# Loading v through the casting software queue, with the transfers of three queues modelled in the planned order

## The chip, the cores and the metric

The kernel runs on one core of a Trainium2 chip. The core has five engines that work side by side, each through its own list of instructions, in that list's order: TensorE (PE, matrix products, with its weight loads shown as PEld), VectorE (DVE), ScalarE (ACT), GpSimd (POOL) and SyncE (SP). Transfers between the chip's memory and its on-chip buffer run on 16 DMA engines that all queues share. SP and ACT issue theirs through hardware queues (q1 and q10 in the profile), POOL through a software queue (q0), whose transfers may change the number type on the way. The metric is device time in microseconds (us), so less is better.

## What is computed

Two things follow each other. First comes a retention layer over q, k and v of shape (4 batches, 8 heads, 768 tokens, 64): a state per head decays by a factor gamma at each token and takes up the outer product of k and v, and q reads it:

```
state = gamma * state + outer(k[t], v[t])
y[t]  = scale * (q[t] @ state)
```

Its output, seen as x of shape (4, 768, 512), goes through an MLP mixer: a token MLP along the tokens (weights 768x256 and 256x768), added to x to give u, and then a channel MLP along the channels (weights 512x1536 and 1536x512), added to u:

```
u   = x + (relu(x^T w_tok1) w_tok2)^T
out = u + relu(u w_ch1) w_ch2
```

Inputs and output are float32. The kernel casts the operands of its matrix products to float16.

## The kernel before

**How the work is tiled.** A *pair* is two heads of one batch, so there are 16 pairs, four in each batch; they are counted from 0 in the order in which they are loaded. The retention of a pair runs in six chunks of 128 tokens. The *front* of a pair (function `front`) does this:

- k is cast to float16 and scaled by a per-token decay (L314 on ACT, L316 on DVE, one instruction a head); q and v are cast as they are (`cast`: L325 on POOL, L323 on ACT).
- k and q are transposed (`turn`). In batches 0 and 1 PE does it (L348) and ACT or DVE moves the result to kT or qT (L356); in batches 2 and 3 a DMA transpose on SP does it (L340).
- PE multiplies k by v for each chunk (L369); DVE accumulates the states (L378, L381), and two copies make them the float16 operand r (L392, L394).
- PE forms the scores of kT and qT, half a sequence at a time (L412); DVE masks them to am (L420).
- PE forms the output from r and qT (L434) and from am and v (L437); ACT or DVE scales it into X (L450, L454), and POOL or DVE casts it to x16 (L467).
- The token MLP follows: x16 by wt1 (L478), ReLU to h1 (L486), h1 by wt2 (L529), added to X (L537). From batch 1 on, u is cast (L545) and transposed to uT, by PE (L566) in batch 1 and by DMA on SP (L556) in batches 2 and 3. In batch 0 PE forms uT itself from wt2, h1 and x16 (L500, L503), and the addition to X comes later.

The *back* of a batch (function `back`) is the channel MLP, in two halves of 384 tokens. One half, a *set* here, is 48 products of wc1 and uT (L598), twelve ReLUs (L612, ACT), 36 products of wc2 (L625), three additions on DVE (L633) and three stores issued by ACT (L639). It needs uT of all four pairs of its batch.

**What sets the order.** Nothing runs while the program is written: every step is first recorded as an `Op` with the engines that could do it, its costs in ns as written in the code, what it depends on, the buffers and PSUM banks that it takes, and a priority. `arrange` (L77) is a list scheduler over these: it keeps a time for each engine, takes among the ops that could start earliest the one of the lowest priority tuple, gives it a start, an end and an engine, and so fixes each engine's list. Priorities of fronts start with 0, batch, pair, step (L297), those of backs with 1 (L587). For transfers it keeps one finish time for the software queue (`wire`) and one for the hardware queues (`ring`), at L139 to L150. PSUM banks 0 to 6 serve the fronts of batch 0, banks 0 to 4 later fronts, 5 to 7 the backs (`BANKS`, L53). Where the plan leaves PE empty in the first 30 us, matmuls on zeros are put in as fillers (L667 to L675).

**Loads.** `load` (L270) puts k, q and v of a pair on SP, as float32, in that order (L282; q of batches 0 and 1 by L279 in longer rows). Each has four buffers. A k or v load has 1536 rows of 256 bytes, so 96 for each DMA engine; q of the first two batches has 512 rows of 768 bytes. The weights are on POOL's software queue (`weight`, L255, issued by L257), which casts them to float16 on the way: wt1 (768 rows), wt2 (256 rows), wc1 and wc2 in three thirds each (512 rows a third). At L664, two of these issues are held back: wt1 until pair 3's q is cast, wc1's first third until pair 3's v is.

Of the kernel before, what the change touches and what calls it, by code (L numbers as in the profile page):

```python
# [17 lines left out]
def kernel(  # L18
# [11 lines left out]
    nc = tc.nc  # L30
# [19 lines left out]

    BUFS = dict(kf=4, qf=4, vf=4, k16=3, q16=3, v16=4, kT=4, qT=4, U=2, r16=3, am=8, X=3, x16=3, h1=4, u16=3,
                uT=3, h2=2, o=4)
# [11 lines left out]
    class Op:  # L64


        def __init__(self, prio, ways, deps=(), takes=(), uses=(), guard=0, dma=0, after=(), behind=None):
            self.prio, self.ways = prio, ways
            self.deps = [d for d in deps if d is not None]
            self.after = [d for d in after if d is not None]  # L70
            self.takes, self.guard, self.dma, self.behind = list(takes), guard, dma, behind
            self.end = self.eng = None
            for s in list(takes) + list(uses):
                s.users.append(self)
            ops.append(self)

    def arrange():  # L77
        free = dict(PE=0, ACT=2500, DVE=0, POOL=400, SP=700)
        wire, ring = [0], [0]
        taken = {t: [] for t in BUFS}  # L80
        bank_of = {i: None for i in range(8)}
        todo, order = list(ops), []

        def freed(slot):
# [6 lines left out]
        while todo:  # L91
# [47 lines left out]
            if op.dma:  # L139
                if eng == "POOL":  # L140
                    wire[0] = max(wire[0], start + 1200) + op.dma
                    op.end = wire[0] + 1000
                elif eng == "ACT":
                    ring[0] = max(ring[0], start + 800) + op.dma
                    op.end = start + 800 + 2 * op.dma + 1500
                else:

                    ring[0] = max(ring[0], start + 800, wire[0]) + op.dma
                    free["SP"] = max(free["SP"], ring[0] - 3600)
                    op.end = ring[0] + 750  # L150
            else:
                op.end = start + way[2]
# [96 lines left out]
    def request(prio, cost, emit, dma, takes=()):  # L249
        o = Op(prio, [("POOL", cost, cost, emit)], [], takes, dma=dma,  # L250
               after=queue[-8:-7], behind=queue[-1] if queue else None)
        queue.append(o)
        return o

    def weight(key, ns, dst, src):  # L255
        def emit():
            nc.gpsimd.dma_start(out=dst, in_=src.rearrange("(i p) j -> p i j", p=P))  # L257
        wops[key] = request((0, -1, 2), 850, emit, ns)

# [10 lines left out]
    def load(b, p):  # L270
        got = []
        for tag, src in (("kf", k), ("qf", q), ("vf", v)):
            s = Slot(tag)

            def emit(s=s, src=src, tag=tag):
                t = tile_of(s, [P, 2, NC, D], FP)
                r = src[b, 2 * p:2 * p + 2]
                if b < XB and tag == "qf":
                    nc.sync.dma_start(out=t.rearrange("p h (f i) d -> p h f (i d)", f=2),  # L279
                                      in_=r.rearrange("h (f p i) d -> p h f (i d)", f=2, p=P))  # L280
                else:
                    nc.sync.dma_start(out=t, in_=r.rearrange("h (c p) d -> p (h c) d", p=P))  # L282
            o = Op((0, b, p), [("SP", 100, 100, emit)], [], [s], dma=1150 if b < XB and tag == "qf" else 1720,
                   after=rows[-3:-2], behind=rows[-1] if rows else None)
            rows.append(o)
            got.append((s, o))
        loads[b, p] = got

    def front(b, p):
        first = b == 0  # L290
        FA = "first" if first else "front"
        n = [0]

        def op(ways, deps=(), takes=(), uses=(), late=0):
            n[0] += 1
            pe = ways[0][0] == "PE"
            pr = (late if late else 0, b, p, n[0])  # L297
            return Op(pr, ways, deps, takes, uses, guard=200 if pe and not first else 0)

# [4 lines left out]
        pc = slice(p * P, (p + 1) * P)  # L304
        (KF, kd), (QF, qd), (VF, vd) = loads[b, p]
        K, Q, V = Slot("k16"), Slot("q16"), Slot("v16")
        KT, QT = Slot("kT"), Slot("qT")

        def emit(e):
            t = tile_of(K, [P, NC, 2, D], F16)  # L310
            for j in range(2):
                h = 2 * p + j
                if e == "ACT":
                    nc.scalar.activation(t[:, :, j], KF.tile[:, j], AF.Copy, scale=gk[:, h:h + 1])  # L314
                else:
                    nc.vector.tensor_scalar(t[:, :, j], KF.tile[:, j], gk[:, h:h + 1], None, ALU.mult)  # L316
        kl = op(either(emit, ACT=(1100, 1180), DVE=(1020, 1080)), [kd, g_op], [K], [KF])

        def cast(slot, src, dep):
            def emit(e):  # L320
                t = tile_of(slot, [P, NC, 2, D], F16).rearrange("p c h d -> p h c d")
                if e == "ACT":
                    nc.scalar.copy(t, src.tile)  # L323
                else:
                    nc.gpsimd.tensor_copy(t, src.tile)  # L325
            ways = either(emit, POOL=(770, 860)) if first else either(emit, POOL=(770, 860), ACT=(780, 860))
            o = op(ways, [dep], [slot], [src])
            casts_of[b, p].append(o)
            return o
        ql = cast(Q, QF, qd)  # L330
        vl = cast(V, VF, vd)

# [3 lines left out]
        def turn(src, dst, dep):  # L336
            if b >= XB:
                def emit():
                    t = tile_of(dst, [P, S], F16)
                    nc.sync.dma_start_transpose(out=t.rearrange("d (c t) -> d c t", t=P),  # L340
                                                in_=flat(src.tile))
                return Op((0, b, p, 0), [("SP", 100, 100, emit)], [dep], [dst], [src], dma=800)
            T = Slot(FA)

            def emit():
                tp = tile_of(T, [P, 1024], F16)
                for c in range(NC):
                    nc.tensor.transpose(tp[:, c * P:(c + 1) * P], src.tile[:, c].rearrange("p h d -> p (h d)"), ident16)  # L348
            t = op(one("PE", (340, 500), emit), [dep, ident_op], [T], [src])

            def emit(e):
                d, o = tile_of(dst, [P, S], F16), T.tile[:, :S]
                if dst is QT:
                    d = d.rearrange("d (f p i) -> d f p i", f=2, i=HC)
                    o = o.rearrange("d (f i p) -> d f p i", f=2, i=HC)
                (nc.scalar.copy if e == "ACT" else nc.vector.tensor_copy)(d, o)  # L356
            return op(either(emit, ACT=act(S), DVE=dve(S, 1.04 if dst is QT else 0.54)),
                      [t], [dst], [T])
        kt = turn(K, KT, kl)
# [5 lines left out]
        def emit():  # L365
            st = tile_of(ST, [P, 512], FP)
            for c in range(NC - 1):
                for j in range(2):
                    nc.tensor.matmul(st[j * D:(j + 1) * D, c * D:(c + 1) * D], K.tile[:, c, j],  # L369
                                     V.tile[:, c, j], start=True, stop=True)  # L370
        pp = op(one("PE", (320, 470), emit), [kl, vl, two_before], [ST], [K, V])
        prev = None
# [29 lines left out]
        for hf in range(2):  # L402
            A = [Slot(FA), Slot(FA)]

            def emit(hf=hf, A=A):
                a = [tile_of(A[j], [P, 512], FP)[:, :HC * P].rearrange("p (i t) -> p i t", t=P)
                     for j in range(2)]
                for i in range(HC):
                    t = slice((hf * HC + i) * P, (hf * HC + i + 1) * P)
                    for j in range(2):  # L410
                        r = slice(j * D, (j + 1) * D)
                        nc.tensor.matmul(a[j][:, i], KT.tile[r, t], QT.tile[r, t],  # L412
                                         start=True, stop=True)
            a = op(one("PE", (300, 420), emit), [kt, qt, two_before], A, [KT, QT])
            for j in range(2):
# [8 lines left out]
        for hf in range(2):  # L424
            Y = Slot(FA)

            def emit(hf=hf, Y=Y):
                y = tile_of(Y, [P, 512], FP)
                R = RS.tile
                for i in range(HC):  # L430
# [5 lines left out]
                    for j in range(2):  # L436
                        nc.tensor.matmul(o[:, j * D:(j + 1) * D], AM[2 * hf + j].tile[:, i],  # L437
                                         V.tile[:, c, j], start=(c == 0), stop=(c == 0 or j == 1))
            y = op(one("PE", (360, 510), emit), am_ops[2 * hf:2 * hf + 2] + [r0, r1, vl], [Y],
# [112 lines left out]
        if b >= XB:  # L552
            def emit():
                if UT.tile is None:
# [3 lines left out]
            e = Op((0, b, p, 99), [("SP", 100, 100, emit)], casts + [None if opens else first_of[b, "uT"]],  # L558
                   [UT] if opens else [], [U16] if opens else [U16, UT], dma=900)
        else:  # L560
# [20 lines left out]
    def back(b):  # L581
        X, UT = Xs[b], UTs[b]
        seq = [0]

        def op(ways, deps=(), takes=(), uses=(), dma=0):
            seq[0] += 1
            return Op((1, b, seq[0]), ways, deps, takes, uses, dma=dma)  # L587
        for sh in range(2):
# [28 lines left out]
            for i in range(HC):  # L617
# [19 lines left out]
                def emit(sh=sh, i=i, O=O):  # L637
                    t0 = (sh * HC + i) * P
                    nc.scalar.dma_start(out=out[b, t0:t0 + P, :], in_=O.tile)  # L639
                op(one("ACT", (60, 60), emit), [ad], [], [O], dma=700)  # L640

    for p in range(NP):
        load(0, p)
    weight("t1", 1900, wt1, moe_w_tok1)
    weight("t2", 1900, wt2, moe_w_tok2)
    for i in range(NW):
        weight(("c1", i), 2600, wc1[i], moe_w_ch1[:, i * FW * P:(i + 1) * FW * P])
    for i in range(NW):
        weight(("c2", i), 2600, wc2[i], moe_w_ch2[i * FW * P:(i + 1) * FW * P])
    for b in range(1, B):  # L650
# [11 lines left out]
    for b in range(B):  # L662
        back(b)
    for key, o in (("t1", casts_of[0, 3][0]), (("c1", 0), casts_of[0, 3][1])):  # L664
        wops[key].deps.append(o)
    order = arrange()
    FILL, F_ON, F_NS = 0.7, 30000, 165  # L667
# [40 lines left out]
```

## Time and profile before

| what | value |
| --- | --- |
| time, median of 13 runs | 228.11 us (226.74 to 231.28) |
| the profiled execution's own time | 228.14 us |
| its span, first to last instruction | 226.2 us |
| PE busy | 203.6 us (90%), 1902 matmuls |
| DVE, ACT, POOL busy | 101.9, 110.4, 53.7 us (45%, 49%, 24%) |
| SP's and the weights' queue, share of 16 engines | q1 61.3%, q0 10.6% |
| outputs' queue | q10 7.8% |
| chain that ended last | PE 53%, DMA 28%, SP's issues 8% |

The span is shorter than the time, because starting and ending a program also counts in the time. A large busy share alone doesn't tell what a change is worth: PE's 90% holds 15.0 us of fillers (L675, 62 matmuls), and stretches in which PE ran at half clock. In a row such as `30.86 2.74 PE L478 MATMUL bank<-x,wt ... x24 [4.53 <-DMA wt<-...]` the numbers are the start, the time covered by the 24 instructions, and in brackets how long the engine was idle before and what ended that wait. In the chain of waits each piece is a start, a length and who held up the end in that stretch. In the slices a digit is the busy share in tenths of one fortieth of the span.

### The profile page before, as it was taken

To read this page: it belongs to the slowest core of one execution; us is meant where nothing else is said; L and a number is where in the kernel's file an instruction comes from. 1 tells how busy PE (TensorE), PEld (TensorE's weight loads), DVE (VectorE), ACT (ScalarE), POOL (GpSimd) and SP (SyncE) were. 2 spreads that over 40 slices of the span, in tenths; PEclk is the share of its full clock that TensorE was granted. 3 is DMA by queue.
4 is the path that set the end of the run, shared out by engine and by line. 5 is a ranking of instruction groups with operands and counts; after the bars stand their busy time and mean duration, and the time that the engine had idled before them with its cause. 6 is when DMAs were issued, how large, how long until landed. Compare 5 with 4: busy or idle time off the path is not lost.

```text
span 226.2 us, 4736 instructions
## 1 busy us (share of the span) xinstructions
PE 203.6 (90%) x1902; PEld 126.2 (56%) x1902; DVE 101.9 (45%) x266; ACT 110.4 (49%) x237; POOL 53.7 (24%) x94
## 2 busy tenths in 40 slices
PE   7987659399999988898699998999999999999993
PEld 3654457378776656665357655654554554645641
DVE  6377812359697858765377457402102102012021
ACT  4476817332889563755336743470460640722700
POOL 1344920303463454343323331300000000000000
PEclk9999967859999999999999999999999999999999
DMA  7999999999999999999999992411202102103012
GB/s 176 243 242 239 214 190 212 205 197 255 199 213 196 174 267 202 209 210 209 188 268 210 176 206 63 130 35 46 93 3 78 61 0 93 49 13 121 5 51 93
DMA packets 93206, 34.13 MB, mean 151 GB/s; under 512 B 81920, under 2 KB 90112, under 8 KB 93184
## 3 DMA queue, kind: packets, MB, share of 16 engines
q1 hardware_dynamic: 85504, 23.60, 61.3%
q0 software_dynamic: 4224, 3.93, 10.6%
q10 hardware_dynamic: 3456, 6.29, 7.8%
q8 instruction: 15, 0.25, 0.5%
q14 instruction: 7, 0.06, 0.1%
HBM read 26.74 MB, written 6.29 MB: 146 GB/s over the span
## 4 chain that ended last, share of the span: by engine, by line
PE 53%; DMA 28%; SPq 8%; POOL 3%; ACT 2%; issue 2%; DVE 2%; POOLq 0%; DVEq 0%; ACTq 0%
PE bank L598 23%; PE bank L625 19%; DMA qf<-in_q_dram 11%; DMA kf<-in_k_dram 7%; DMA qT<-q 7%; SPq L282 4%; PE bank L529 3%; PE bank L478 2%; DMA vf<-in_v_dram 2%; SPq L279 2%; PE bank L412 2%; SPq L340 2%; POOL v L325 1%; PE bank L348 1%; ACT h L612 1%
## 5 line engine op out<-in xcount | busy, mean ns | idle before, releaser
L612 ACT ACTIVATE h<-bank 128x384 f16<-128x384 f32 x96 | 46.1, 489 | 45.4 <-DVE o L633 32.0
L598 PE MATMUL bank<-uT,wc 128*128 128x384 f16 x384 | 68.2, 326 | 0.0
L625 PE MATMUL bank<-wc,h 128*128 128x512 f16 x288 | 67.2, 379 | 0.0
L598 PEld LDWEIGHTS <-wc 128*128 128x128 f16 x384 | 35.8, 98 | 22.1
L633 DVE TENSOR_TENSOR o<-X,bank 128x512 f32<-128x512 f32 x24 | 16.4, 685 | 67.8 <-PE bank L625 67.8
L625 PEld LDWEIGHTS <-h 128*128 128x128 f16 x288 | 26.8, 98 | 28.8 <-issue 0.3
L420 DVE TENSOR_TENSOR am<-bank,mask 128x384 f16<-128x384 f32 x64 | 33.0, 550 | 17.4 <-PE bank L412 17.0
L450 ACT ACTIVATE X<-bank,gy 128x192 f32<-128x192 f32 x44 | 15.6, 415 | 19.1 <-PE bank L437 11.5
L314 ACT ACTIVATE k<-kf,gk 128x384 f16<-128x384 f32 x28 | 15.7, 607 | 9.4 <-DMA kf<-in_k_dram 7.2
L537 DVE TENSOR_TENSOR X<-X,bank 128x384 f32<-128x384 f32 x32 | 16.1, 548 | 8.7 <-PE bank L529 8.2
L325 POOL CAST q<-qf 128x768 f16<-128x768 f32 x13 | 10.8, 829 | 36.3 <-DMA qf<-in_q_dram 34.0
L478 PE MATMUL bank<-x,wt 128*128 128x128 f16 x192 | 15.2, 237 | 4.5 <-DMA wt<-in_moe_w_tok_dram 4.5
L381 DVE SCALAR_TENSOR_TENSOR U<-U,gp,bank 128x64 f32<-128x64 f32 x64 | 17.7, 276 | 1.2
L467 POOL CAST x<-X 128x384 f16<-128x384 f32 x28 | 14.1, 511 | 13.5 <-DVE X L454 10.1
L478 PEld LDWEIGHTS <-wt 128*128 128x128 f16 x192 | 13.3, 107 | 6.5 <-DMA wt<-in_moe_w_tok_dram 4.7
L545 POOL CAST u<-X 128x384 f16<-128x384 f32 x23 | 11.3, 510 | 22.7 <-DVE X L537 22.7
L325 POOL CAST v<-vf 128x768 f16<-128x768 f32 x14 | 11.6, 830 | 18.7 <-DMA vf<-in_v_dram 14.2
L675 PE MATMUL bank<-zero 128*128 128x384 f16 x62 | 15.0, 379 | 1.2 <-DVE zero L205 1.2
L412 PE MATMUL bank<-qT,kT 64*128 64x128 f16 x192 | 10.0, 223 | 5.8 <-DMA qT<-q 5.2
L529 PE MATMUL bank<-h,wt 128*128 128x128 f16 x192 | 14.2, 225 | 0.0
L437 PE MATMUL bank<-v,am 128*128 128x64 f16 x192 | 13.5, 193 | 0.0
L529 PEld LDWEIGHTS <-wt 128*128 128x128 f16 x192 | 12.1, 101 | 2.2 <-issue 0.2
(57 smaller groups left out, 155.8 us busy)
## 6 DMA issues: line engine op xcount, KB each, us to landing
kf<-in_k_dram SPq DMA_DIRECT2D x16, 384.0 KB, 6.5
qf<-in_q_dram SPq DMA_DIRECT2D x16, 384.0 KB, 5.8
vf<-in_v_dram SPq DMA_DIRECT2D x16, 384.0 KB, 5.9
out_dram<-o ACTq DMA_DIRECT2D x24, 256.0 KB, 2.0
wc<-in_moe_w_ch_dram POOLq DMA_DIRECT2D x6, 512.0 KB, 18.5
wt<-in_moe_w_tok_dram POOLq DMA_DIRECT2D x2, 384.0 KB, 8.8
kT<-k SPq DMA_TRANSPOSE x8, 5.3
qT<-q SPq DMA_TRANSPOSE x8, 5.4
```

The lines of the kernel that those rows point to most:

```text
L314: nc.scalar.activation(t[:, :, j], KF.tile[:, j], AF.Copy, scale=gk[:, h:h + 1])
L325: nc.gpsimd.tensor_copy(t, src.tile)
L381: nc.vector.scalar_tensor_tensor(U[:, c], U[:, c - 1], gp[:, p:p + 1], o, ALU.mult, ALU.add)
L420: nc.vector.tensor_tensor(am, src, m, ALU.mult)
L450: nc.scalar.mul(X.tile[:, half(hf), h * D:(h + 1) * D], yv[:, :, j * D:(j + 1) * D], gy[:, h:h + 1])
L478: nc.tensor.matmul(acc[:, jt * P:(jt + 1) * P], wt1[:, i, jt * P:(jt + 1) * P], X16.tile[:, i], start=(i == 0), stop=(i == NC - 1))
L529: nc.tensor.matmul(acc[:, i * P:(i + 1) * P], wt2[:, jt, t], H1.tile[:, jt], start=(jt == 0), stop=(jt == NJ - 1))
L537: nc.vector.tensor_tensor(xo, xo, T2.tile[:, :HC * P].rearrange("p (i d) -> p i d", d=P), ALU.add)
L598: nc.tensor.matmul(acc[:, :SH], w[:, ct, (ft % FW) * P:(ft % FW + 1) * P], UT.tile[:, ct, sh * SH:(sh + 1) * SH], start=(ct == 0), stop=(c ...
L612: nc.scalar.activation(H2.tile[:, ft], A.tile[:, :SH], AF.Relu)
L625: nc.tensor.matmul(A.tile, H2.tile[:, ft, i * P:(i + 1) * P], wc2[ft // FW][:, ft % FW], start=(ft == 0), stop=(ft == NF - 1))
L633: nc.vector.tensor_tensor(o, X.tile[:, sh * HC + i], A.tile, ALU.add)
```

## The change

It has these parts:

1. **v** is no longer loaded by SP as float32 and cast by POOL or ACT. POOL issues its load on the software queue, straight into a float16 buffer (`v16`, now six instead of four; `vf` is gone). The v loads of batch 0 come first on that queue, then the weights, then the other v loads. v16 is laid out by head and chunk instead of by chunk and head, and the products that read it name it so.
2. **The model of transfers.** A transfer is recorded as rows per DMA engine and ns per row, both written in the code. After each planning pass, `wires` sends the transfers of SP, POOL and ACT through the engines together, row by row in turns, and gives each a latency, which the next pass uses. Eight passes are made, and the best of the last five by its own estimate is emitted.
3. **Token weights.** wt1's issue is held until pair 2's q is cast (before: pair 3's). wc1's first third waits for the last part of pair 3's q.
4. **First front by stage.** In batch 0 the priority is step before pair instead of pair before step, so the four pairs go through a stage together.
5. **Halves.** k's scaling of the two heads, and pair 3's q cast and transposed copies, become separate ops (`parts`), which two engines may share. Score products wait for their half of kT and qT.
6. **Buffers**: x16 five instead of three, h1 five instead of four.

The diff, cut to its core:

```diff
-    BUFS = dict(kf=4, qf=4, vf=4, k16=3, q16=3, v16=4, kT=4, qT=4, U=2, r16=3, am=8, X=3, x16=3, h1=4, u16=3,
+    BUFS = dict(kf=4, qf=4, k16=3, q16=3, v16=6, kT=4, qT=4, U=2, r16=3, am=8, X=3, x16=5, h1=5, u16=3,
                 uT=3, h2=2, o=4)
...
+    GEN = dict(SP=20, ACT=20)
+    FIRST = dict(SP=600, POOL=1300, ACT=600)
+    LAND = dict(SP=800, POOL=1000, ACT=1500)
+
+    def wires(order):
...
+            round_ = sum(o.dma[1] for k, o in on)
+            for k, o in on:
+                step = dt / round_
+                if o.made > t:
+                    step = min(step, dt / GEN.get(k, 8))
+                left[k] -= step
...
-                if eng == "POOL":
-                    wire[0] = max(wire[0], start + 1200) + op.dma
-                    op.end = wire[0] + 1000
...
+                op.end = start + (op.lat or 2200 + op.dma[0] * op.dma[1])
+                if eng == "SP":
+                    free["SP"] = max(start + 550, gens[-2])
+                    gens.append(max(start + 550, gens[-1]) + op.dma[0] * GEN["SP"])
...
-               after=queue[-8:-7], behind=queue[-1] if queue else None)
+               after=queue[-6:-5], behind=queue[-1] if queue else None)
...
-        for tag, src in (("kf", k), ("qf", q), ("vf", v)):
+        for tag, src in (("kf", k), ("qf", q)):
...
+        s = Slot("v16")
+
+        def emit(s=s):
+            nc.gpsimd.dma_start(out=tile_of(s, [P, 2, NC, D], F16),
+                                in_=v[b, 2 * p:2 * p + 2].rearrange("h (c p) d -> p (h c) d", p=P))
+        got.append((s, request((0, b, p), 1040, emit, (96, 15), [s])))
...
-            pr = (late if late else 0, b, p, n[0])
+            pr = (late, b, n[0], p) if first else (late, b, p, n[0])
...
+        kl = parts(emit, dict(ACT=(540, 610), DVE=(490, 540)), [kd, g_op], K, KF, ([0], [1]))
...
+        if last:
+            ql = parts(emit, dict(POOL=(400, 510), ACT=(440, 510), DVE=(490, 540)), [qd], Q, QF,
+                       (slice(0, 1), slice(1, 2)))
...
-        ql = cast(Q, QF, qd)
-        vl = cast(V, VF, vd)
...
-    for key, o in (("t1", casts_of[0, 3][0]), (("c1", 0), casts_of[0, 3][1])):
+    for key, o in (("t1", casts_of[0, 2][0]), (("c1", 0), casts_of[0, 3][-1])):
         wops[key].deps.append(o)
-    order = arrange()
+    best = None
+    for turn in range(8):
+        order = arrange()
+        wires(order)
+        t = max(o.end for o in order)
+        if turn > 2 and (best is None or t < best[0]):
+            best = t, [(o, o.start, o.end, o.eng, o.emit, [s.bank for s in o.takes]) for o in order]
```

What it makes of the lists: POOL's first transfers are the v loads of pairs 0 to 3, then three q casts and two x casts, then wt1 and wt2, then the six thirds of wc1 and wc2, then v of pairs 4 to 9. SP's list is k and q of the pairs in turn, with the DMA transposes from pair 8 on. On PE the four pairs of batch 0 come first with 53 fillers instead of 62, then the token MLP and uT of batch 0, and then a whole set of batch 0's back, with only the transposes, scores and L369 of the first pairs of batch 1 between; four sets, instead of five, stand behind the last front. PE's other matmuls are the same in number and kind.

## The prediction

> **What bounds the kernel now.** I read the page's slices first: TensorE (PE), the clock it was granted, and the DMA engines, in 40 slices of 5.65 us.
>
> ```profile
> PE   7987659399999988898699998999999999999993
> PEclk9999967859999999999999999999999999999999
> DMA  7999999999999999999999992411202102103012
> ```
>
> PE is full from slice 8 (45 us) on; slices 3 to 7 hold 7, 6, 5, 9, 3, and the clock dips there. DMA is full from 6 to 136 us. Busy time by stretch comes next. I cut at 53.3 us, where the first channel-MLP matmul (L598) runs, and at 146.0, where the last front is done:
>
> ```profile
> core 0: us, PE busy (x) PEld busy (x) DVE busy (x) ACT busy (x) POOL busy (x), PEclk, DMA share, GB/s
> 0.00:53.30 53.30, 41.34 (x472) 29.49 (x473) 29.03 (x97) 28.11 (x59) 18.11 (x33) 0.87 1.17 214
> 53.30:146.00 92.70, 85.70 (x1022) 56.62 (x1020) 61.77 (x154) 53.83 (x120) 34.61 (x60) 1.00 1.16 200
> 146.00:222.60 76.60, 76.54 (x412) 40.14 (x410) 10.42 (x17) 28.48 (x58) 0.97 (x2) 1.00 0.14 51
> ```
>
> After 146 PE never waits: five sets of 48 L598 (7.80 us in the chain of waits) and 36 L625 (7.77). Counted with the chain's pieces (six transposes 0.34 us, L412 x12 0.54, L369 x10 0.28, L437 and L434 x17 0.62, L478 x12 and L529 x12 0.67 each, a half of L500/L503 0.49), PE needs 179.8 us in all, fillers left out. Its last matmul ends at 222.6, so 42.8 us are lost: in the first stretch 53.3 less 20.8 of work = 32.5, in the second 92.7 less 82.4 = 10.3. The chain of waits and PE's timeline say where:
>
> ```profile
> 24.40 18.75 DMA qf<-in_q_dram
> ...
> 43.31 0.84 POOL q L325
> ...
> 44.19 0.82 PE bank L348 x6
> ...
> 133.46 3.94 DMA qT<-q
> ```
>
> ```profile
> 25.84 0.50 PE L348 MATMUL bank<-ident,k 128*128 128x128 f16 x6
> 30.86 2.74 PE L478 MATMUL bank<-x,wt 128*128 128x128 f16 x24 [4.53 <-DMA wt<-in_moe_w_tok_dram]
> ```
>
> PE waits 4.53 us for the token weights wt1 and 3.52 us for the sixth pair's q. After each wait the granted clock is half (0.51 from 30.9 to 36.5, 0.50 from 44.2 to 50.1): 2.8 and 2.9 us more. Why wt1 is late stands in POOL's timeline:
>
> ```profile
> 15.86 0.83 POOL L325 CAST q<-qf 128x768 f16<-128x768 f32 x1 [2.20 <-DMA qf<-in_q_dram]
> 16.63 0.51 POOL L467 CAST x<-X 128x384 f16<-128x384 f32 x1
> ...
> 18.37 0.51 POOL L467 CAST x<-X 128x384 f16<-128x384 f32 x1
> 21.43 0.83 POOL L325 CAST q<-qf 128x768 f16<-128x768 f32 x1 [2.55 <-DMA qf<-in_q_dram]
> ...
> 22.65 1.69 POOL L257 DMA_DIRECT2D wt<-in_moe_w_tok_dram  x2
> ```
>
> It is issued behind the fourth pair's q; by the packet records its first packet runs at 25.36, and it lands 8.2 us after its issue. Last, the DMA view, of 36 to 50 us (weights on q0, SP's loads on q1) and of 76 to 78 us (SP's loads alone); columns are packets, MB, share of 16 engines:
>
> ```profile
> q0 software_dynamic: 2092, 2.08, 87.2%
> q1 hardware_dynamic: 2094, 0.79, 32.7%
> ```
>
> ```profile
> q1 hardware_dynamic: 1735, 0.44, 138.4%
> ```
>
> The queues take turns, packet by packet: a pair costs 14 us x 16 / 2093 = 107 ns. That is how pair 5's q, issued at 24.40, takes 18.75 us. Alone, a 256-byte packet costs 2 us x 16 / 1735 = 18.4 ns, so a k or v load (96 packets an engine) 1.77 us. All weights need 28.1 us, from 25.36 to 53.5.
>
> **The change, part by part.** Pairs are counted from 0.
>
> *wt1 behind pair 2's q.* That q landed at 15.8 and can land no earlier now: by then SP has sent three k and three q, and q0 two v and most of a third, as before. POOL's order in the changed program puts pair 0's two x casts ahead of pair 2's q cast; they need both halves of its X, so both of its L450 evictions, and PE puts L369 of pair 1 (which needs v1) ahead of pair 0's outputs. The second x cast ran at 18.37 behind a v cast that is gone; I put it at 17, pair 2's cast to 17.8, and wt1 at 18.0, 4.7 us earlier. Ends: 16.7 (nothing but the landed q waits) and 22.7 (no gain). wt1 lands at 26.2 instead of 30.9, and the weights flow from 20.7 to 48.8.
>
> *The rest of batch 0.* From wt1's landing to the first L598 before: 22.45 us = 12.6 work + 3.5 wait + 5.7 half clock + 0.6. Now PE's order has 10.2 us of work there and no pair-5 q; I keep one half-clock stretch (2.8) and the 0.6: 26.2 + 13.6 = 39.8. The first third of wc1 landed at 36.5 (issue 25.1, 11.4 to landing) and moves to 31.8, so it is in time.
>
> *PE's new order.* One whole set of batch 0 (48 L598, 36 L625) now stands ahead of most of batch 1's fronts. From L598's start to the point with as much work left before the tail as before had at 53.3 (82 us) are 18.0 us: 57.8. Its data: pair 5's q is the 256th q1 packet per engine since 20.7, and the weights are 48+16+192 = 256 q0 packets, so it lands at 49.4 and, cast, meets its transpose due at 51.4. v4 stands behind the weights on q0: 48.8 + 96 pairs x 36.8 ns + 1 = 53.3, for L369 due at 54.9. The tail is now four sets, 62.0 us.
>
> *v by the casting queue.* It removes 16 casts (14 of 0.83 us on POOL, two on ACT), of which the chain of waits shows 1% (POOL v L325), inside the 10.3 us, and adds 16 POOL issues; by the rows 704 (wt2, 256 descriptors), 775 (wc, 512) and 993 ns (wt1, 768), 1536 cost 1.2 to 1.7 us. POOL, 53.7 us busy of 226, hides them. The program lets eight software transfers be out: the issue of v9 waits for wc2's first third (wc1's lands at 31.8, the next three 3.5 us apart: 42), with pair 6's q cast behind it, due at 51. Later issues wait for a v slot, so for an output of six pairs before; behind them stand x and u casts of the same pairs, which are late enough.
> A packet of 256 bytes read and cast isn't in the trace. Below: SP's transposes, 1122 packets in a us (80 to 81), 14.3 ns. Above: the software queue's records, median 60, 96 and 134 ns for 512, 1024, 1536 bytes landed; back on that line 128 bytes cost 32. I take 18.4, the plain packet that reads the same run.
> [...]
> [...]
>
> *Stages ranked, halves, more buffers, 53 fillers for 62.* They set the order used above; k's halves were two instructions already. I add nothing for them.
>
> **The sum.** From 57.8 PE needs 81.7 us: last front not before 139.5. DMA after 48.8: ten k 17.7, ten q 16.7 (two at 1.29), twelve v 21.2, 20 transposes at 0.75 15.0, eleven outputs at 0.735 8.1 = 78.7. Before, the same kinds made 74.0 and took 83.9 (53.5 to 137.4, the last qT), 1.134 times; so now 89.2, to 138.0. From the last qT to the last front it was 8.6 us: 146.6 if q0's v fill none of SP's idle spots. Between 139.5 and 146.6 I take the middle, 143.0. Then 62.0, and 3.6 for the last addition and store: span 208.6. The profiled run took 228.14 for a span of 226.2; with these 1.9 the forecast is **211 us** (17 below the profiled time, which equals the median 228.11).
>
> **Rivals.**
> - *PE's work alone sets the end* (v packets at 14.3 ns, SP's spots filled): 139.5 + 62.0 + 3.6 + 1.9 = 207. For it: 10.3 us lost were partly SP blocked behind v. Against: DMA is as full. 20%.
> - *The input stretch keeps its length*: 92.7 from 57.8, 150.5, so 218. For it: the chain there is DMA. Against: DMA is some loads ahead at 57.8. 15%.
> - *wt1 isn't earlier*, pair 0's X being late through v1: 57.8 becomes 62.5, PE's bound 144.2, DMA's 151.3, middle 147.8: 215. 14%.
> - *Slower: v's packet costs what the software queue's line gives*, 32 ns, on q0, whose turns SP's loads share. 16 x 96 x 13.6 ns = 21 us on the DMA path: 232. It decides from 30 ns on, where 17 us are gone. For: each software packet of the trace is dearer than a plain one. Against: they move more. 10%.
>
> My forecast has 40% (own range 208 to 214); 1% is left for anything else. The range of 203.5 to 221 leaves out the dear packet. About 0.5% is what a measurement of this kernel can tell from no change: faster 0.89, same 0.01, slower 0.10.
>
> **What would show it.** wt's issue near 18.0 and first L478 near 26.2; first L598 near 39.8; no 3.5 us wait for q; q0 packets of 128 bytes near 18 ns; last L529 near 143; then 62 us of PE without a gap. A v packet over 30 ns, v landing after its L369 is due, or PE waiting at L412 for qT past 145 make it wrong.

## The result and the profile after

The changed kernel takes **216.68 us** (median of 14 runs, 215.74 to 218.08) against 228.13 for the kernel before (62 runs); the ratio is 0.951, with a 95% interval of 0.949 to 0.953. Medians here are of all runs, while the ratios and their intervals leave out runs more than 1.5% above a kernel's fastest. The forecast was 211, with a range of 203.5 to 221: the sign and the range held, but 11.4 us were gained and not 17. The question is where the other 5.7 us went.

The profiled execution took 216.76 us for a span of 215.0. Its page, in 40 slices of 5.38 us:

```profile
PE   7897999997999999629999899999999999999993
PEclk9998899999999999988999999999999999999999
DMA  7999999999999999999999998544202012012012
```

The hole that was in slices 3 to 7 of PE's row is nearly gone. A new one, 6 and 2, stands in slices 16 and 17 (86 to 97 us), followed by a dip of the clock. The transfers fill slices 1 to 23, as before. The busy time by stretch, cut at the point of equal remaining work (57) and at the last front's end (149.3):

```profile
core 0: us, PE busy (x) PEld busy (x) DVE busy (x) ACT busy (x) POOL busy (x), PEclk, DMA share, GB/s
0.00:57.00 57.00, 50.57 (x536) 32.94 (x537) 31.69 (x103) 36.10 (x73) 23.10 (x35) 0.97 1.35 202
57.00:149.30 92.30, 85.90 (x1026) 57.01 (x1025) 62.25 (x154) 53.34 (x123) 31.73 (x53) 0.98 1.26 171
149.30:211.40 62.10, 61.99 (x335) 32.50 (x332) 8.46 (x14) 23.52 (x48) 0.97 (x2) 1.00 0.15 55
```

The first and the last stretch came out as predicted (57.8 and 62.0). The middle one took 92.3 us where 85.2 had been put. Of PE's waits after 40 us, its timeline shows two that matter (in brackets the idle time before, and what ended it):

```profile
54.09 0.35 PE L439 MATMUL bank<-v,k 128*64 128x64 f16 x10 [1.63 <-DMA v<-in_v_dram]
```
```profile
95.15 3.29 PE L668 MATMUL bank<-uT,wc 128*128 128x384 f16 x10 [5.67 <-ACT h L682]
```

The second is the hole. ACT's timeline around it shows that ACT wasn't working; it stood at a store (L709) from 88.1 to 94.2:

```profile
85.45 0.34 ACTq L709 DMA_DIRECT2D out_dram<-o  x1
...
87.57 0.49 ACT L682 ACTIVATE h<-bank 128x384 f16<-128x384 f32 x1 [0.94 <-PE bank L668]
94.20 0.36 ACTq L709 DMA_DIRECT2D out_dram<-o  x1
94.61 1.25 ACT L682 ACTIVATE h<-bank 128x384 f16<-128x384 f32 x3 [6.55 <-DMA qf<-in_q_dram]
```

A store of an output waiting for a load of q makes no sense by the data: the store needs only DVE's sum, which was there at 87.6, and that q (pair 11's) isn't cast until 102.9. The chain of waits names the same load:

```profile
88.06 1.15 SPq L403
...
89.30 4.82 DMA qf<-in_q_dram
...
94.20 0.36 ACTq L709
```

The trace's records explain it. They give each transfer the number of the semaphore that it adds to when it is done. The 80 transfers that SP and ACT issue carry eight numbers (101, 103 to 106, 116 to 118), each ten times, and 65 of the 80 issues come behind a wait for their own number. Pair 11's q load, issued at 89.30, carries 116, and so does this store: ACT's wait for 116 ends at 94.15, just after the load's landing at 94.13, and the store was issued at 94.20. The cast of that q (L386 on POOL) waits for 116 too.

The ReLUs (L682) behind the store in ACT's list stood with it: the one at 87.57 ended at 88.06, and the next ran at 94.61. They free PE's banks, so PE stood as well. After the 5.67 us of idling the granted clock was 0.50 from 94.8 to 98.2, which cost some 1.6 us more (ten L668 took 3.2 us and not 1.6). Together that is 7.3 us, and 92.3 - 85.2 = 7.1 were missing.

### The profile page after: what moved, and what is told of

Read it like the earlier page. It is cut to its first block, busy times and chain, and to the rows that moved or that the text cites. A ratio compares the mean times of both kernels' runs of the same rounds, so it can differ in the third digit from the quotient of the medians.

```text
span 215.0 us, 4706 instructions
## 1 busy us (share of the span) xinstructions
PE 198.5 (92%) x1893; PEld 122.5 (57%) x1893; DVE 103.0 (48%) x269; ACT 113.0 (53%) x244; POOL 55.8 (26%) x90
## 4 chain that ended last, share of the span: by engine, by line
PE 70%; DMA 19%; ACT 3%; SPq 3%; DVE 2%; issue 1%; POOL 1%; ACTq 0%
PE bank L695 27%; PE bank L668 25%; DMA v<-in_v_dram 11%; DMA qf<-in_q_dram 8%; PE bank L599 4%; PE bank L548 4%; PE bank L482 2%; PE bank L507 2%; PE bank L504 2%; PE bank L439 2%; SPq L322 1%; SPq L325 1%; ACT X L520 1%; PE bank L412 1%; PE bank L756 1%
## 5 line engine op out<-in xcount | busy, mean ns | idle before, releaser
L668 PE MATMUL bank<-uT,wc 128*128 128x384 f16 x384 | 70.6, 331 | 5.7 <-ACT h L682 5.7
L682 ACT ACTIVATE h<-bank 128x384 f16<-128x384 f32 x96 | 46.0, 490 | 51.4 <-DVE o L703 24.0
L668 PEld LDWEIGHTS <-wc 128*128 128x128 f16 x384 | 35.9, 99 | 29.1 <-issue 7.3
L333 POOL DMA_DIRECT2D v<-in_v_dram x16 | 16.6, 1041 | 17.6 <-PE bank L507 8.6
L520 ACT ACTIVATE X<-bank,gy 128x192 f32<-128x192 f32 x50 | 17.8, 418 | 5.6 <-PE bank L507 5.4
L537 POOL CAST x<-X 128x384 f16<-128x384 f32 x23 | 11.9, 519 | 32.6 <-DVE X L524 16.2
L615 POOL CAST u<-X 128x384 f16<-128x384 f32 x23 | 11.2, 507 | 25.9 <-DVE X L607 23.1
L386 POOL CAST q<-qf 128x768 f16<-128x768 f32 (+1 forms) x12 | 9.8, 813 | 18.0 <-DMA qf<-in_q_dram 18.0
L376 ACT ACTIVATE k<-kf,gk 128x384 f16<-128x384 f32 x22 | 12.8, 610 | 2.6 <-DMA kf<-in_k_dram 2.5
L507 PEld LDWEIGHTS <-am 128*128 128x128 f16 x192 | 12.4, 98 | 3.0 <-DVE am L490 0.9
L462 ACT ACTIVATE r<-U 64x320 f16<-64x320 f32 x26 | 12.2, 467 | 3.4 <-DVE U L451 3.1
L548 PE MATMUL bank<-x,wt 128*128 128x128 f16 x192 | 13.4, 219 | 0.0
L599 PEld LDWEIGHTS <-wt 128*128 128x128 f16 x192 | 11.7, 98 | 2.8 <-issue 0.9
## 6 DMA issues: line engine op xcount, KB each, us to landing
wc<-in_moe_w_ch_dram POOLq DMA_DIRECT2D x6, 512.0 KB, 16.6
```

What stands on the lines that cost most here:

```text
L333: nc.gpsimd.dma_start(out=tile_of(s, [P, 2, NC, D], F16), in_=v[b, 2 * p:2 * p + 2].rearrange("h (c p) d -> p (h c) d", p=P))
L520: nc.scalar.mul(X.tile[:, half(hf), h * D:(h + 1) * D], yv[:, :, j * D:(j + 1) * D], gy[:, h:h + 1])
L548: nc.tensor.matmul(acc[:, jt * P:(jt + 1) * P], wt1[:, i, jt * P:(jt + 1) * P], X16.tile[:, i], start=(i == 0), stop=(i == NC - 1))
L599: nc.tensor.matmul(acc[:, i * P:(i + 1) * P], wt2[:, jt, t], H1.tile[:, jt], start=(jt == 0), stop=(jt == NJ - 1))
L668: nc.tensor.matmul(acc[:, :SH], w[:, ct, (ft % FW) * P:(ft % FW + 1) * P], UT.tile[:, ct, sh * SH:(sh + 1) * SH], start=(ct == 0), stop=(c ...
L682: nc.scalar.activation(H2.tile[:, ft], A.tile[:, :SH], AF.Relu)
```

## The experiments

Two theories stood at first. *Store*: the wait above is the whole loss. *Transfers*: the loads are late whatever waits for them, and if that wait is taken away another comes. Ratios are against the kernel before, run beside each kernel on the same chip.

**One store on POOL.**

```diff
-                    nc.scalar.dma_start(out=out[b, t0:t0 + P, :], in_=O.tile)
+                    e = nc.gpsimd if (b, sh, i) == (0, 1, 2) else nc.scalar
+                    e.dma_start(out=out[b, t0:t0 + P, :], in_=O.tile)
```

> The changed kernel with one output store (the sixth, third block of batch 0's second half) issued by POOL in place of ACT; nothing else. In the changed kernel that store waited on ACT from 87.6 to 94.2 us, ACT's ReLUs stood behind it, and PE idled 5.67 us and then ran 3.4 us at half clock. Theory 'store': the wait is the whole loss; the idle and the half clock go, the last front ends up to 7.4 us earlier (149.3 to 142), and the time is 209 to 210 us. Theory 'transfers': SP's transfers are late in any case; PE then meets the tenth pair's scores at 91, and their qT, issued at 91.6, lands at 96; PE idles there instead and 2 us are gained, 214.7 us. No gain at all, 216.7, if the store was not what ACT waited for.

Measured: 218.0 us, ratio 0.955 (0.951 to 0.959): no gain. The 5.67 us are gone, and PE has no wait over 0.7 us from 55 to 107 us. Then the same thing happens at another store. This is the chain of waits of this kernel, and the PE row that it ends in:

```profile
103.99 7.43 DMA kf<-in_k_dram
...
111.50 0.34 ACTq L710
...
111.88 0.39 ACT h L556
112.28 0.04 issue
112.32 1.44 PE bank L599 x12
```
```profile
112.32 1.44 PE L599 MATMUL bank<-h,wt 128*128 128x128 f16 x12 [3.58 <-ACT h L556]
```

PE idles 3.58 us, and the clock is at half from 110.5 to 117.3. It is also at half from 55.9 to 59.3, behind a wait of 1.87 us for v, which the changed kernel's profiled execution doesn't show. So the number expected by *store* failed, but the same kind of wait was met a second time, at a store that stood until this k load had landed (at 111.42).

**Half of v**, on the changed kernel and with the one store moved. These kernels leave out the second head of v in batches 1 to 3, in its load and in both products that read it (the cut shows one), so a part of the computation is changed.

```diff
+            n = 2 * NC if b == 0 else NC
-            nc.gpsimd.dma_start(out=tile_of(s, [P, 2, NC, D], F16),
-                                in_=v[b, ...].rearrange("h (c p) d -> p (h c) d", p=P))
+            nc.gpsimd.dma_start(out=tile_of(...).rearrange("p h c d -> p (h c) d")[:, :n],
+                                in_=v[b, ...].rearrange("h (c p) d -> p (h c) d", p=P)[:, :n])
...
-                                     V.tile[:, j, c], ...
+                                     V.tile[:, j if b == 0 else 0, c], ...
```

> The changed kernel, but the twelve v loads of batches 1 to 3 bring one head of the pair instead of two (48 packets an engine instead of 96), and the second head's products use the first head's v; that part of the computation is changed. Theory 'transfers': 12 x 48 x 15 ns = 8.6 us of transfers go from the stretch of 57 to 149 us, SP's loads come earlier, and most of it is gained: 209 to 211 us. Theory 'store': v's transfers are hidden; the time moves only as far as the one q load that the store waits for lands earlier, and PE still idles there: 213 to 216.7 us.

> Both edits: one head of v in batches 1 to 3 (part of the computation changed as before) and the sixth store issued by POOL. Theory 'store': as the store edit alone, 209 to 210 us, since v's transfers cost nothing once the store is out of ACT's way. Theory 'transfers': 207 us or so, several us below the store edit alone, with PE never waiting between 57 us and the last front.

Measured: 208.03 us, ratio 0.914 (0.910 to 0.917), and with the store moved 208.46, 0.915 (0.912 to 0.918). With half of v's packets in batches 1 to 3, 8.6 us are gained, and the store adds nothing to that. The last front ends at 140.2, against PE's own bound of 139.5 in the prediction. SP's timeline shows how v reaches SP. Here are the issues that lead to pair 11's q, the changed kernel first, then half of v; the second number is the time that SP spent on one issue:

```profile
72.84 5.56 SPq L403 DMA_TRANSPOSE kT<-k  x1
78.46 0.56 SPq L325 DMA_DIRECT2D qf<-in_q_dram  x1
79.13 4.00 SPq L403 DMA_TRANSPOSE qT<-q  x1
83.23 0.53 SPq L325 DMA_DIRECT2D kf<-in_k_dram  x1
83.86 5.35 SPq L403 DMA_TRANSPOSE kT<-k  x1
89.30 0.53 SPq L325 DMA_DIRECT2D qf<-in_q_dram  x1
```
```profile
71.80 1.31 SPq L404 DMA_TRANSPOSE kT<-k  x1
73.17 0.56 SPq L325 DMA_DIRECT2D qf<-in_q_dram  x1
73.84 2.07 SPq L404 DMA_TRANSPOSE qT<-q  x1
76.01 0.53 SPq L325 DMA_DIRECT2D kf<-in_k_dram  x1
78.32 1.21 SPq L404 DMA_TRANSPOSE kT<-k  x1
79.63 0.53 SPq L325 DMA_DIRECT2D qf<-in_q_dram  x1
```

The three transposes hold SP for 14.9 us with all of v and for 4.6 with half of it. Pair 11's q is issued 9.7 us earlier, and from 60 to 140 us PE is busy for 79.87 of 80. All 24 stores are still issued by ACT here, at 0.34 us each. So issuing a store on ACT cost PE next to nothing by itself here (0.13 us idle of 80); a store that had to wait there cost 5.67 us.

**All stores of batches 0 and 1 on POOL** (the same edit with `b < 2` as its condition).

> The changed kernel with all twelve stores of batches 0 and 1 issued by POOL in place of ACT. With the sixth alone moved, PE ran without a wait up to 107 us, and then the same thing came at the next-but-two store: ACT waited at it until 111.5 for a k load issued at 104.0, PE idled 3.58 us and then ran at half clock. Theory 'store' as it stands now (late loads reach PE through the stores in ACT's order): no store waits on ACT any more, PE idles little, and the time is 209 to 212 us; what is left is the wait for the late k itself, 2 to 3 us. Theory 'transfers' (the loads set the pace whatever carries them): another wait of like size comes in its place, at the next scores, 215 to 217 us.

Measured: 212.93 us, ratio 0.927 (0.920 to 0.934), below the changed kernel's interval: **the lowest ratio of the kernels that compute the whole reference** (by the median, one that follows, 212.8, is level with it). The last front ends at 144.8 instead of 149.3. *Store* holds for 3.8 us by the medians (216.7 to 212.9) and for 5.5 by the ratios (0.951 to 0.927). The edit does two things that the runs don't separate: these stores no longer wait on ACT, and they no longer share semaphores with SP's own issues (in the changed kernel's trace POOL's transfers carry other numbers, 107 to 114). What is left is this, and another 1.29 us for a qT at 126:

```profile
54.25 0.35 PE L439 MATMUL bank<-v,k 128*64 128x64 f16 x10 [2.60 <-DMA v<-in_v_dram]
```
```profile
core 0: us, PE busy (x) PEld busy (x) DVE busy (x) ACT busy (x) POOL busy (x), PEclk, DMA share, GB/s
51.70:54.20 2.50, 0.00 (x0) 0.00 (x0) 0.34 (x1) 0.61 (x1) 0.00 (x0) 1.00 1.61 162
55.40:58.80 3.40, 3.40 (x10) 1.28 (x9) 2.22 (x7) 0.00 (x0) 1.90 (x3) 0.53 1.67 206
60.00:120.00 60.00, 59.59 (x712) 39.83 (x710) 45.47 (x111) 41.18 (x93) 26.62 (x43) 1.00 1.44 200
```

**One part undone or done alone.** First the guard of wt1, by itself on the kernel before, and put back in the changed kernel, without and with the stores moved:

```diff
-    for key, o in (("t1", casts_of[0, 2][0]), ...
+    for key, o in (("t1", casts_of[0, 3][0]), ...
```

> The kernel before with one line changed: the token weights wt1 are held back until the third pair's q is cast, not the fourth's. By my prediction's step wt1 lands up to 4.7 us earlier, and the last front follows by as much if PE's wait on wt1 is what sets it: 223.4 us. If the loads of SP set the end of the input stretch, the weights in front of them only swap places: 228 us.

> The changed kernel with the one line of the guard put back: wt1 is held until the fourth pair's q is cast. By my prediction's rival 'wt1 not earlier' the point of equal remaining work comes up to 4.7 us later and the time is 4 us higher, 220 to 221 us. If PE's start is given back later in the input stretch, where loads set the pace, it is 217 us.

> The changed kernel with both edits: the guard put back to the fourth pair's q, and the twelve stores of batches 0 and 1 issued by POOL. The guard alone cost nothing (216.9 against 216.7). If its 4 us were given back at the stores, whose waits came when SP's loads landed, they appear once no store waits: 216 to 217 us against the 212.9 of the stores alone. If the loads take the guard's gain in any case, 213 us.

Measured: alone 227.36 us, ratio 0.996 (0.992 to 1.000); put back 216.93, 0.949 (0.942 to 0.955); put back with the stores moved 212.8, 0.934 (0.930 to 0.938). By the medians the earlier wt1 is worth 1.0, 0.2 and -0.1 us, by the ratios 0.9, -0.5 and 1.6, and in the last two the intervals overlap. It does what it says, and most or all of it is given back. In the changed kernel with the old guard PE waits for wt1 and the first L668 comes 6.4 us later (37.22 in the changed kernel):

```profile
31.42 4.07 PE L548 MATMUL bank<-x,wt 128*128 128x128 f16 x48 [3.04 <-DMA wt<-in_moe_w_tok_dram]
...
43.58 0.65 PE L668 MATMUL bank<-uT,wc 128*128 128x384 f16 x3
```

But then it doesn't wait for v at 54, and the stores' waits, which end when loads land, cost it 0.86 and 2.47 us instead of 5.67. That the gain was lost at the stores alone would have made the kernel with both edits take 216 to 217 us; it took 212.8. There the first L668 comes at 41.30 (36.41 with the stores alone moved), and yet the last front ends at 145.0 (144.8). With the new guard the lead goes into the 2.60 us for v and the half clock behind that.

Next, batch 0's ranking by pair again, without and with the stores moved:

```diff
-            pr = (late, b, n[0], p) if first else (late, b, p, n[0])
+            pr = (late, b, p, n[0])
```

> The changed kernel with batch 0's fronts ranked pair by pair as before, not stage by stage; the rest is as changed, and the program's own planning is done anew with it. I added nothing for the ranking, so 216.7 us is expected. If the ranking is what put a whole channel-MLP set of batch 0 ahead of the fronts of batch 1, the first L668 comes later and the time is 220 us or more.

> The changed kernel with batch 0 ranked pair by pair and the twelve stores of batches 0 and 1 issued by POOL. With the ranking alone PE lost 4.42 us at one store that waited for a k load. Without stores on ACT that goes and the time is 211 to 212 us; if the late loads make PE wait elsewhere, 214 to 216 us.

Measured: 215.99 us, 0.943 (0.936 to 0.949), and 214.88, 0.944 (0.939 to 0.949). By itself the ranking shows no gain: the intervals meet, and ranked by pair the kernel loses 4.42 us at a store that waited for a k load, as the changed kernel does for a q load. With the stores moved, ranking by stage is the better one, by 2.0 us of the medians, and the intervals don't meet, though they rest on three and four runs. My 211 to 212 failed: ranked by pair, PE waits 2.33 us for a q cast at 21.7, runs at half clock behind it (20.3 to 27.1), and waits 1.93 us for v at 59.

Then v on SP, as float32 with casts, all else as changed (SP's window of loads was set back to three with it):

```diff
-        for tag, src in (("kf", k), ("qf", q)):
+        for tag, src in (("kf", k), ("qf", q), ("vf", v)):
...
+            (nc.scalar.copy if e == "ACT" else nc.gpsimd.tensor_copy)(t, VF.tile)
+        vl = op(either(emit, POOL=(770, 860)) if first else either(emit, POOL=(770, 860), ACT=(780, 860)), ...
```

> The changed kernel with v loaded again by SP as float32 and cast by POOL or ACT; guard, ranking, buffers and model stay as changed. By my prediction v's move was worth what lies between DMA's end and PE's in the stretch from 57 to the last front: without it 224 us or so (4.7 us gained by the guard alone). If v's move is worth nothing by itself, 217 us; if the guard is worth nothing by itself, as the kernel before with the new guard shows (227.4), then 227 us.

Measured: 222.39 us, ratio 0.963 (0.955 to 0.972). The kernel is slower than the changed one, but by how much is open: 5.7 us by the medians, 2.8 by the ratios, whose intervals allow 0.5 to 5.2 and of which this one rests on two runs. So v's move is worth some of the 11.4 us, and the other parts together are worth the larger part by the ratios and half by the medians. Which of model, halves, buffers and ranking gives it with v on SP wasn't split further.

**Two attempts at less.** v of batch 1's first pair asked for ahead of the wc2 thirds (it is the fifth v load of the queue; the expectation calls it the seventh), and batch 2's transposes of u by PE; both with the stores moved.

```diff
+    load(1, 0)
     for i in range(NW):
         weight(("c2", i), 32, 97, wc2[i], ...)
```
```diff
-        if b >= XB:
+        if b >= XB + 1:
             ...
                 nc.sync.dma_start_transpose(out=UT.tile[:, p].rearrange("d (c t) -> d c t", t=P),
```

> The changed kernel with the twelve stores of batches 0 and 1 issued by POOL, and the seventh v load (v4 in the wait list is the first pair of batch 1) asked for ahead of the last three weight loads instead of behind them. With the stores alone PE still waits 2.60 us for that v at 54 and then runs at half clock for some 2.5 us. If that wait sets the time, 5 us go: 208 us. If the loads behind set it, 212 to 213 us; if the wc2 weights now come late for the first L695, above 213.

> The changed kernel with the twelve stores of batches 0 and 1 issued by POOL, and batch 2's four transposes of u made by PE (six 128x128 transposes and a copy by ACT or DVE each) in place of SP's DMA. Nothing of the computation changes. Taken from the stores alone (212.9 us): theory 'transfers', the DMA engines' work still sets the end of the input stretch: 4 x 0.75 = 3.0 us of transfers go and PE gets 4 x 0.34 = 1.4 us, so 1.5 us or so are gained, 211.4 us. Theory 'PE', that little but PE's own work is left after the stores were moved: 1.4 us or more are lost, 214.3 us.

Measured: 213.62 us, 0.937 (0.932 to 0.941), and 213.84, 0.934 (0.929 to 0.939). Neither gains. In the first, PE waits 1.03 us for that v instead of 2.60 and the clock stays whole there, but it then waits 1.56, 1.42 and 0.84 us for qT, at 104, 121 and 133. In the second it still waits 2.30 us for v at 55 and 1.79 for a qT at 115, runs at half clock from 114.9 to 118.3, and has four sets of six transposes more to do (1.4 us by 0.34 each). Their intervals overlap that of the stores alone, so they are inconclusive on a loss, but the 208 us of the first (if the wait for v set the time) and the 211.4 of the second (*transfers*) lie outside their intervals (0.932 x 228.0 = 212.5, 0.929 x 228.3 = 212.0).

## Why the prediction was right or wrong

- **wt1.** Right. Its issue came at 19.03 (predicted 18.0), it landed and the first L548 ran at 26.43 (26.2). What was wrong is its price: the rival "wt1 isn't earlier" gave 4 us for losing it, and by their intervals the first two guard runs leave at most 1.8 and 1.5. The step behind that price, that the end of the middle stretch moves with its start, is refuted by them; in the third, with the stores moved, the intervals reach to 4.1, but the last front stays in place.
- **First L668**, 37.22 against 39.8. I kept a stretch at half clock (2.8 us) behind wt1's landing. There was none there. One of 3.4 us came earlier, from 19.7 to 23.1 (granted 0.50), where PE would have waited for wt1 anyway.
- **Equal remaining work**, 57.0 against 57.8. v4 landed at 54.0 (53.3 predicted) and was needed at 52.5, not at 54.9, since PE was early: a wait of 1.63 us that the sum didn't have, and one of the prediction's own signs against itself ("v landing after its L369 is due"). That the point came out within 0.8 us is partly luck: a start 2.6 us early and this wait worked against each other.
- **v's packet**, taken at 18.4 ns. In the DMA view from 84.5 to 85.3 it flows alone, so 0.8 us x 16 / 976 = 13.1 ns, which is below even my lower bound of 14.3:

```profile
q0 software_dynamic: 976, 0.12, 244.0%
```

  From 74 to 75 both queues run, and a packet of either takes 16 / 973 us = 16.4 ns:

```profile
q0 software_dynamic: 506, 0.06, 99.5%
q1 hardware_dynamic: 467, 0.12, 68.8%
```

  506 packets in 99.5% of 16 us are 31.5 ns a record, right at the 32 ns of the slower rival. But the records of q0 and q1 sum to 168%, and alone q0's came to 244%, so more than one is under way at once in an engine. So my test "a v packet over 30 ns makes it wrong" was itself wrong. A record's length isn't a price; packets counted per time are.
- **POOL's issues** of v took 1.04 us (mean of 16, 16.6 us in all), less than the 1.2 to 1.7 put.
- **The last front, 143.0**, is the step that failed: 149.3. The sum of transfers held (last qT landed at 136.6, predicted 138.0), but the last front came 12.7 us behind it and not 5.0 (143.0 less 138.0), since PE had fallen behind. PE's bound held too (half of v reached it, 208 us against the rival's 207). That the end lies halfway between the two bounds was a choice without a reason from the rows, and it put the coupling of the engines at nothing: with all of v three transposes held SP for 14.9 us (4.6 with half of it), so a q load was issued late, at 89.30; a store on ACT waited for it by the shared semaphore, 116, to 94.15; ReLUs, banks and PE followed (5.67 us), and then the half clock (94.8 to 98.2). The prediction reckoned with such a limit on the software queue ("The program lets eight software transfers be out"), and the trace has at most eight under way there: POOL's wait ahead of the issue of v9 ended at 42.79, just after wc2's first third had landed at 42.77. It left out such a wait on the transfers of SP and ACT. With the stores off ACT the last front is at 144.8, 1.8 us from my term, and the time at 213.
- **Tail**, 62.0, and the 3.7 after it: right. The 1.9 from span to time was 1.8.
- **The rivals.** "The input stretch keeps its length" has the measured length (92.3 against 92.7) and the nearest time, 218, but not for its reason. Without the stores on ACT the stretch is shorter although the transfers are the same. In the other direction it isn't empty either: with half of v it is 83.2 us, so v's transfers set a part of what is left.

Two things stay open: why SP's transposes took up to 5.56 us to issue with all of v under way (the effect is shown, its mechanism isn't), and how the 4.9 us (3.1 by the ratios) between the stores moved (212.9) and half of v (208.0) divide between the wait for v at 54 and the later ones.

## What to carry to other kernels

In the changed kernel a store waited not only for its data, there at 87.6, but also for an earlier load on its semaphore, to 94.15, so read the semaphores in the waits of stores before putting them on an engine whose other work is urgent. When such a store is moved away, look for the next one like it: one store moved gained nothing, twelve gained 3.8 us by the medians. A step that comes earlier is worth only what the next late thing leaves of it, so price a shift by what its successors wait for at the new time.

## What the runs showed of the hardware

- In the changed kernel records of small casting packets last 31.5 ns (74 to 75 us) and 32 ns (84.5 to 85.3), but alone, in the second of these stretches, they flow at 13.1 ns each: their records sum to 244% of the 16 engines' time, so they overlap.
- In the changed kernel the granted clock falls to half at 19.73 and 94.82 us and rises at 23.14 and 98.23 by the trace's clock records: each half-clock stretch lasts 3.41 us, and the two falls lie 22 times that apart. In the kernel before, the half-clock stretches go from 29.60 to 36.43 and from 43.25 to 50.08, 6.83 us or twice 3.41 each, and the two falls lie four times 3.41 apart. With one store moved the clock is at half from 110.5 to 117.3, 6.8 us.
- In the 3.41 us before these falls PE was busy for 0.56 and 0.00 of the time in the changed kernel, and for 0.04 and 0.24 in the kernel before. But the same share was 0.44 in the changed kernel from 87.99 to 91.41, and 0.43 in the kernel before from 111.52 to 114.93, and full clock followed, so in these two traces the share alone doesn't tell when the clock falls. Nor does the length of one idle gap: in the changed kernel the fall at 19.73 came behind a gap of 1.04 us, while with the old guard and the stores moved a gap of 2.34 us left the clock at 1.00 from 20 to 40 us:

```profile
19.14 0.51 PE L412 MATMUL bank<-ident,q 128*128 128x128 f16 x6 [1.04 <-POOL q L386]
```
```profile
30.77 2.85 PE L548 MATMUL bank<-x,wt 128*128 128x128 f16 x48 [2.34 <-DMA wt<-in_moe_w_tok_dram]
```
